# The first batch's mixing side by side, and the first block's second layer by halves of its weights

## The chip, the cores and the metric

The kernel runs on one core of one Trainium2 chip. The metric is device time of one launch, in microseconds (us). A core has TensorE (PE, matmuls; PEld are its weight loads), VectorE (DVE), ScalarE (ACT), GpSimd (POOL) and SyncE (SP, here only an issuer of transfers). Transfers between device memory and the on-chip buffer run on 16 DMA engines; in this kernel GpSimd issues the loads of inputs, SyncE the small ones and the outputs. TensorE writes its results to PSUM, eight banks of 128 partitions by 2 KB; VectorE and ScalarE copy them out.

## The reference

Attention with a few extra "beacon" keys per head, and on its output a mixing over the sequence of low rank (rank 32) followed by a two-layer network over the channels. Eight batches, eight heads of 64, 576 tokens, 16 beacons, 512 channels, 2048 in the hidden layer:

```python
k_all = np.concatenate([beacon_k, k], axis=2)
v_all = np.concatenate([beacon_v, v], axis=2)
scores = scale * np.matmul(q, k_all.transpose(0, 1, 3, 2))
causal[:, Nb:] = np.triu(np.ones((S, S), dtype=bool), k=1)
scores = np.where(causal, -1000000000.0, scores)
...
a /= a.sum(-1, keepdims=True) + 1e-09
x = np.matmul(a, v_all)            # heads side by side: (B, S, 512)
xt = x.transpose(0, 2, 1)
h = xt @ U @ V                     # U: 576 x 32, V: 32 x 576
u = x + h.transpose(0, 2, 1)
out = u + np.maximum(u @ w_ch1, 0.0) @ w_ch2
```

## The kernel before

*Tiling.* The 576 tokens of a batch are cut into five tiles (112, 128, 128, 128, 80 tokens), the 512 channels into four blocks of 128, the heads into four pairs per batch. Pairs are numbered through all batches: 0 to 3 are the first batch's, 4 to 7 the second's, 8 to 11 the third's. The network runs over blocks of 512 rows of the (8 x 576) rows; the first block therefore lies wholly in the first batch.

*Attention.* For a pair, q and k are regrouped on VectorE into a tile `pr` (`regroup`, copies at L268, the beacons at L270), turned by TensorE (`tps`, L275 or L281), copied out of PSUM into `qT` and `kT` (L308, L313), multiplied into scores (`sps`, L348 or L382), exponentiated by ScalarE (`expt`), masked by VectorE and multiplied with V of the attention (`po`, L397). VectorE then writes the normalised result into `xb` (L405, L406).

*Mixing.* The head of the mixing multiplies U with `xb` into `qtp` (32 rows of rank by channels), VectorE copies that to an f16 tile, and the correction multiplies it with V. The results accumulate in PSUM upon the turned x (`ups` for tokens 0 to 495, `uend` for the last 80) and are copied into `uT`, channels by tokens. For batches from the second on (`mix_units`) all four channel blocks stand side by side: the head writes them into four column groups of 32 (L434), and the correction reads them in four row groups of 32 (L459). For that `Vsb` holds V four times, in rows 0, 32, 64 and 96 on, and `Vend` the last 80 columns of V in one row group per block, with zeros elsewhere. The first batch has its own `first_mix` (L481), which does the blocks in two sets, 0 and 1, then 2 and 3: `head(c0, n)` takes both blocks of a set as one matmul of 256 columns per token tile (L489); `begin` brings the turned x into PSUM; `rest` multiplies each block with V (L506) and copies out.

*Small inputs.* `small_loads` (L162) lets SyncE read U and V as f32 into one tile. `cast`, called later, lets GpSimd write them as f16 (`Usb`, L176; `Vsb`, L177); SyncE then copies V to the other row groups (L181) and its end into `Vend` (L182). GpSimd issues the loads of the second batch, of w1 (four quarters) and of w2 (two halves, L195) around that call, in the order of the code, and then the third batch's loads (`load_batch(2)`).

*Network.* `mlp_units` makes a list of steps for a block of 512 rows: 16 g-steps (first layer, `gps`, L534, one PSUM bank each, relu out to `gT`) and then 16 c-steps (second layer, `cps`, L560): step (i, part) multiplies rows i x 128 on with four of the sixteen hidden slices; four parts fill a bank, the fourth is followed by the copy `ob` (VectorE for even i in the first block, L577, ScalarE for odd i, L575) and the transfer out. Hidden slices 0 to 7 read the first half of w2, 8 to 15 the second.

*Order.* The order of the work on each engine is that of the code (`manual_schedule`, L808), written out by hand. The steps of the network stand in a list, `queue`, and `fill(n)` takes n off it between pieces of attention ("f" in the lines of `play` takes one). After the second batch's attention, `mix(1)` puts the second batch's mixing among the 16 c-steps of the first block: head, c-step, corrections (`most`), three c-steps, end part, and from then on a c-step and an empty place by turns for four c-steps. Then come, at L905 to L909: eight steps of the queue, the regrouping of pairs 8 and 9 (six copies on VectorE, which need the third batch's k and q), eight more steps, and a line that begins with the turning of pair 8's q, a step, the turning of its k, a step, and pair 8's scores.

Of the kernel before, what the change touches and what calls it, by code (L numbers as in the profile page):

```python
# [11 lines left out]
F32 = mybir.dt.float32  # L12
# [6 lines left out]
P = 128  # L19
# [11 lines left out]
def kernel(  # L31
# [13 lines left out]
    nc = tc.nc  # L45
    B, H, S, D = q.shape
    Nb = beacon_k.shape[2]
    DM = H * D
    R = moe_U.shape[1]
# [12 lines left out]
    nq = [min(S, P * (j + 1) - Nb) - q0[j] for j in range(NC)]  # L62
    NT = NC
    QM, NL = q0[NT - 1], nq[NT - 1]
# [97 lines left out]
    def small_loads():  # L162

        f = utp.tile([P, NT * R + S], F32, name="small", tag="ut")
        nc.vector.memset(f[0:1, 0:1], 0.0)
        uf, vf = f[:, 0 : NT * R].rearrange("p (j r) -> p j r", r=R), f[0:R, NT * R :]
        nc.sync.dma_start(out=uf[: nq[0], 0, :], in_=moe_U[0 : nq[0], :])
        nc.sync.dma_start(
            out=uf[:, 1 : NT - 1, :], in_=moe_U[q0[1] : QM, :].rearrange("(j p) r -> p j r", p=P)
        )  # L170
        nc.sync.dma_start(out=uf[:NL, NT - 1, :], in_=moe_U[QM:S, :])
        nc.sync.dma_start(out=vf, in_=moe_V)

        def cast():
            for rr, jj in ((nq[0], slice(0, 1)), (P, slice(1, NT - 1)), (NL, slice(NT - 1, NT))):
                nc.gpsimd.tensor_copy(out=Usb[:rr, jj, :], in_=uf[:rr, jj, :])  # L176
            nc.gpsimd.tensor_copy(out=Vsb[0:R, :], in_=vf)  # L177
            for cc in range(NCC):
                rs = ds(R * cc, R)
                if cc:  # L180
                    nc.sync.dma_start(out=Vsb[rs, :], in_=Vsb[0:R, :])  # L181
                nc.sync.dma_start(out=Vend[rs, cc, :], in_=Vsb[0:R, QM:S])  # L182

        return cast

# [295 lines left out]
    def first_mix(xb):  # L481

        qts = outp.tile([P, DM], F16, name="qfirst", tag="ob")
        cell = {}

        def head(c0, n):
            qtp = pst([R, P * n], F32, name="qtp")
            for j in range(NT):
                nc.tensor.matmul(  # L489
                    qtp, Usb[: nq[j], j, :], xb[: nq[j], j, ds(P * c0, P * n)], start=(j == 0), stop=(j == NT - 1)  # L490
                )
            nc.vector.tensor_copy(out=qts[0:R, ds(P * c0, P * n)], in_=qtp)
            emptying(qtp)

        def begin(c0, cs, n=2):
            for cc in cs:
                cell[cc] = pst([P, QM], F32, name="ups")
                x_into(xb, cell[cc], cc, list(range(NT - 1)), 0, True)
                if cc == c0:
                    cell["end"] = pst([P, n, NL], F32, name="uend")  # L500
                x_into(xb, cell["end"][:, cc - c0, :], cc, [NT - 1], QM, cc == c0)

        def rest(c0, n, copies, end):
            for at in (0, QM):
                for i in range(n):
                    nc.tensor.matmul(  # L506
                        cell["end"][:, i, :] if at else cell[c0 + i], qts[0:R, ts(c0 + i, P)],
                        Vsb[0:R, at : S if at else QM], start=False, stop=True, skip_group_check=True,
                    )
            for cc, copy in zip(range(c0, c0 + n), copies):  # L510
                copy(out=uT[:, cc, 0:QM], in_=cell[cc])
                emptying(cell[cc])
            end(out=uT[:, ds(c0, n), QM:S], in_=cell["end"])
            emptying(cell["end"])

        return head, begin, rest

    def mlp_units(t0, n, dst, flip, turned=True, last=False):


        units = []
        gT = {}
        held = {}

        def turn():
            ut = utp.tile([P, 4, DM], F16, name="ut", tag="ut")
            for cc in range(NCC):
                nc.sync.dma_start_transpose(out=ut[:, :, ts(cc, P)], in_=uT[:, cc, ds(t0, 4 * P)])
            gT["u"] = ut

        def g_part(dc, upto):
            g, done = held.get(dc) or (pst([P, 512], F32, name="gps"), 0)
            for cc in range(done, upto):
                nc.tensor.matmul(  # L534
                    g[:, 0:n], w1[:, cc, ts(dc, P)], uT[:, cc, ds(t0, n)], start=(cc == 0), stop=(cc == NCC - 1)
                )
            held[dc] = g, upto

        def g_unit(dc):
            if dc == 0:  # L540
                gT["t"] = gtp.tile([P, NDC, 512], F16, name="gT", tag="gT")
                if turned:
                    turn()
            g_part(dc, NCC)
            g, _ = held.pop(dc)
            if (dc % 3 if not turned else (dc + flip) % 2 or dc in (5, 6, 7)):
                nc.scalar.activation(out=gT["t"][:, dc, 0:n], in_=g[:, 0:n], func=AF.Relu)  # L547
            else:
                nc.vector.tensor_scalar_max(out=gT["t"][:, dc, 0:n], in0=g[:, 0:n], scalar1=0.0)  # L549
            emptying(g)  # L550

        cps = {}

        def c_unit(i, part):
            m = min(P, n - P * i)
            if part == 0:
                cps["t"] = pst([P, DM], F32, name="cps")
            ps = cps["t"]
            for dc in range(4 * part, 4 * part + 4):
                nc.tensor.matmul(  # L560
                    ps[:m, :], gT["t"][:, dc, ds(P * i, m)], w2[:, dc, :], start=(dc == 0),
                    stop=turned and dc == NDC - 1, skip_group_check=True,
                )
            if part == 3:
                ob = outp.tile([P, DM], F32, name="ob", tag="ob")
                if not turned:
                    for cc in range(NCC):
                        nc.tensor.matmul(
                            ps[:m, ts(cc, P)], uT[:, cc, ds(t0 + P * i, m)], ident, start=False, stop=True,
                            skip_group_check=True,  # L570
                        )
                if turned:
                    nc.vector.tensor_tensor(out=ob[:m, :], in0=ps[:m, :], in1=gT["u"][:m, i, :], op=ALU.add)  # L573
                elif i % 2:
                    nc.scalar.activation(out=ob[:m, :], in_=ps[:m, :], func=AF.Copy)  # L575
                else:
                    nc.vector.tensor_copy(out=ob[:m, :], in_=ps[:m, :])  # L577
                emptying(ps)
                nc.sync.dma_start(out=dst(i, m), in_=ob[:m, :])

        def c_half(i, part):
            hs = ds(DM // 2 * (part // 2), DM // 2)
            if part % 2 == 0:
                cps["t"] = pst([P, DM // 2], F32, name="cph")
            for dc in range(NDC // 2 * (part % 2), NDC // 2 * (part % 2 + 1)):
                nc.tensor.matmul(  # L586
                    cps["t"], gT["t"][:, dc, ts(i, P)], w2[:, dc, hs], start=(dc == 0), stop=(dc == NDC - 1)
                )
            if part % 2:
                ob = outp.tile([P, DM // 2], F32, name="oh", tag="ob")  # L590
                nc.vector.tensor_tensor(out=ob, in0=cps["t"], in1=gT["u"][:, i, hs], op=ALU.add)
                emptying(cps["t"])
                nc.sync.dma_start(out=dst(i, P)[:, hs], in_=ob)

        units += [lambda dc=dc: g_unit(dc) for dc in range(NDC)]
        for i in range((n + P - 1) // P):
            c = c_half if last and i == n // P - 1 else c_unit
            units += [lambda i=i, part=part, c=c: c(i, part) for part in range(4)]
        return units, g_part


# [206 lines left out]
    with tc.manual_schedule(engines={ENG.PE, ENG.Activation, ENG.DVE, ENG.SP, ENG.Pool}):  # L808
# [60 lines left out]
        head, begin, rest = first_mix(xbs[0])  # L869
        feed(0)  # L870
        part = state["part"]
# [7 lines left out]
        rest(0, 2, (act_copy, act_copy), act_copy)  # L879
        av = av_of(3)  # L880
        av[0]()
        av[1]()
        begin(2, (2,))
        part(D0, 2)
        part(D1, 2)
        head(2, 2)
# [100 lines left out]
        for p in range(NP1, NP):  # L987
            b, c = divmod(p, NH2)
# [78 lines left out]
    with tc.If(n_bad != 0, label="general"):  # L1067
        with tc.For_i(0, B, 1) as bi:
            L = qk_tiles()
            qT = qkt.tile([P, NH2, S], F16, name="qT", tag="qT")  # L1070
            xb = xbp.tile([P, NT, DM], F16, name="xb", tag="xb")
# [11 lines left out]
            for t0 in range(0, S, 512):  # L1083
                n = min(512, S - t0)
# [32 lines left out]
```

## Time and profile before

| | |
|---|---|
| median of 3 runs | 350.42 us (349.91 to 350.76) |
| the profiled execution's own time | 350.22 us |
| its span, first to last instruction | 348.6 us |
| TensorE busy | 341.6 us, 98% |
| VectorE, ScalarE, GpSimd busy | 190.5, 163.5, 98.0 us |
| moved by the DMA engines | 41.88 MB |

A profile is of one execution. Rows of the chain give start, length and what; rows of a timeline give start, length, engine, line, operation, output and inputs, shape and count, and in brackets how long the engine had been idle and what ended that. Lines (L...) are those of the kernel's file. Ends of matmuls are modelled, so a row's length reaches a little beyond the next start; differences of starts are safer.

### The profile page before, as it was taken

The page shows a single profiled execution, that of the slowest core. Times are in us where ns is not written, and L with a number is a line of the kernel's source. Part 1 is how long each engine was busy: PE and PEld are TensorE (multiplying, and loading weights), DVE is VectorE, ACT ScalarE, POOL GpSimd, SP SyncE. Part 2 cuts the span into 40 slices and gives each one's busy share as a digit, 9 for nine tenths or more (in the row PEclk, how much of TensorE's full clock was granted, in tenths as well). Part 3 has the DMA queues.
Part 4 walks back from the last instruction along what each step waited for, and adds up shares of the span by engine and source line. Part 5 has one row for each costly group of instructions (what it writes and reads, how often), then busy time and mean ns, then how long its engine had stood idle before and what let it go on. Part 6 is the DMA issues. An engine that isn't in the chain of part 4 may idle for free.

```text
span 348.6 us, 7792 instructions
## 1 busy us (share of the span) xinstructions
PE 341.6 (98%) x3084; PEld 173.0 (50%) x3084; DVE 190.5 (55%) x492; ACT 163.5 (47%) x358; POOL 98.0 (28%) x137
## 2 busy tenths in 40 slices
PE   8999999999999999999999999999999999999995
PEld 3565564555554455444554545445445444444443
DVE  5776964789875653654565456535655542323311
ACT  5957851578823665167614753494434203302300
POOL 8885713653505547303830140000000000000000
PEclk9999999999999999999999999999999999999999
DMA  9999999999999999991999799613123314013011
GB/s 168 128 181 182 157 196 181 222 145 144 131 147 144 159 152 127 172 190 8 141 134 192 124 107 132 179 44 68 63 75 47 68 63 120 2 60 105 17 65 65
DMA packets 146635, 41.88 MB, mean 120 GB/s; under 512 B 131488, under 2 KB 142080, under 8 KB 146592
## 3 DMA queue, kind: packets, MB, share of 16 engines
q0 software_dynamic: 87440, 18.18, 71.6%
q1 hardware_dynamic: 58928, 22.84, 36.3%
q8 instruction: 26, 0.43, 0.6%
q10 hardware_dynamic: 224, 0.30, 0.3%
q14 instruction: 17, 0.14, 0.2%
HBM read 37.37 MB, written 9.44 MB: 134 GB/s over the span
## 4 chain that ended last, share of the span: by engine, by line
PE 88%; DMA 7%; DVE 2%; ACT 1%; issue 0%; POOL 0%
PE gps L534 35%; PE cps L560 33%; PE po L397 8%; PE sps L382 6%; DMA st<-in_q_dram 6%; ACT expt L354 1%; PE tps L275 1%; PE sps L348 1%; PE cph L586 1%; DMA stq<-in_q_dram 1%; PE qtp L434 1%; PE tps L281 1%; DVE qT L308 1%; DVE pr L268 1%; PE ups L459 1%; DVE kT L308 0%
## 5 line engine op out<-in xcount | busy, mean ns | idle before, releaser
L534 PE MATMUL gps<-uT,w 128*128 128x512 f16 x576 | 136.0, 379 | 0.1
L560 PE MATMUL cps<-w,gT 128*128 128x512 f16 x560 | 130.9, 379 | 0.1
L388 ACT ACTIVATE expt<-sps 128x496 f16<-128x496 f32 x192 | 82.5, 534 | 71.6 <-PE sps L382 71.6
L547 ACT ACTIVATE gT<-gps 128x512 f16<-128x512 f32 x86 | 50.9, 622 | 78.8 <-PE gps L534 78.7
L534 PEld LDWEIGHTS <-w 128*128 128x128 f16 x576 | 51.8, 98 | 58.0 <-issue 2.4
L560 PEld LDWEIGHTS <-gT 128*128 128x128 f16 x560 | 50.9, 98 | 59.4 <-issue 6.5
L549 DVE TENSOR_SCALAR gT<-gps 128x512 f16<-128x512 f32 x58 | 39.9, 690 | 41.6 <-PE gps L534 39.9
L573 DVE TENSOR_TENSOR ob<-cps,ut 128x512 f32<-128x512 f32 x31 | 21.4, 691 | 48.3 <-PE cps L560 47.5
L218 POOL DMA_DIRECT2D vs<-in_v_dram x50 | 39.6, 807 | 17.0 <-PE po L397 4.8
L397 PEld LDWEIGHTS <-expt 128*128 128x128 f16 (+1 forms) x960 | 36.2, 98 | 12.8 <-issue 1.0
L397 PE MATMUL po<-vs,expt 128*128 128x65 f16 (+1 forms) x960 | 38.9, 194 | 0.1
L406 DVE TENSOR_TENSOR xb<-po,rec 128x320 f16<-128x320 f32 x64 | 31.5, 491 | 2.2
L324 DVE TENSOR_TENSOR expt<-expt,bigmask 128x512 f16<-128x512 f16 x58 | 24.3, 418 | 6.7 <-ACT expt L388 6.7
L354 ACT ACTIVATE expt<-sps 128x496 f16<-128x496 f32 (+1 forms) x64 | 27.0, 606 | 0.7 <-PE sps L348 0.6
L405 DVE RECIPROCAL rec<-po 128x5 f32<-128x5 f32 x64 | 12.1, 188 | 26.9 <-PE po L397 26.6
L382 PE MATMUL sps<-qT,kT 64*128 64x80 f16 (+4 forms) x288 | 23.3, 281 | 0.1
L200 POOL DMA_DIRECT2D vs<-in_beacon_v_dram x8 | 4.3, 536 | 57.2 <-PE po L397 57.2
L646 POOL DMA_DIRECT2D st<-in_q_dram x20 | 16.9, 863 | 7.2 <-DMA vs<-in_v_dram 4.3
L382 PEld LDWEIGHTS <-kT 64*128 64x128 f16 x288 | 9.8, 94 | 18.3 <-issue 14.4
L646 POOL DMA_DIRECT2D st<-in_k_dram x20 | 16.9, 868 | 3.3 <-DMA st<-in_q_dram 2.9
L446 DVE TENSOR_TENSOR uT<-ups,uT 128x496 f16<-128x496 f32 x24 | 14.5, 667 | 5.0 <-PE ups L459 5.0
L308 DVE COPY qT<-tps 128x576 f16<-128x576 f16 (+1 forms) x16 | 11.8, 735 | 3.5 <-PE tps L281 2.3
(97 smaller groups left out, 162.4 us busy)
## 6 DMA issues: line engine op xcount, KB each, us to landing
out_dram<-ob SPq DMA_DIRECT2D x35, 256.0 KB, 2.3
vs<-in_v_dram POOLq DMA_DIRECT2D x18, 128.0 KB, 7.3
w<-in_moe_w_ch_dram POOLq DMA_DIRECT2D x4, 512.0 KB, 6.9
w<-in_moe_w_ch_dram POOLq DMA_DIRECT2D x2, 1024.0 KB, 14.3
st<-in_k_dram POOLq DMA_DIRECT2D x12, 128.0 KB, 8.9
st<-in_q_dram POOLq DMA_DIRECT2D x12, 128.0 KB, 9.4
st<-in_k_dram POOLq DMA_DIRECT2D x2, 576.0 KB, 13.1
st<-in_q_dram POOLq DMA_DIRECT2D x2, 576.0 KB, 15.9
```

The source lines that it names most:

```text
L218: nc.gpsimd.dma_start(out=dst[a : a + nq[j], j, :, :], in_=src[hs, ds(q0[j], nq[j]), :].rearrange("h p d -> p h d"))
L324: nc.vector.tensor_tensor(out=e4, in0=e4, in1=bigmask, op=ALU.min)
L354: nc.scalar.activation(out=ex[i][:, ds(SLOT * g, gw[g])], in_=ps[g, i][:, 0 : gw[g]], func=AF.Exp, scale=scale)
L382: nc.tensor.matmul(ps[p, g, i][:, ds(o, w)], kT[hp, c, ds(P * ch, P)], qT[hp, c, ds(qa, w)], start=True, stop=True,)
L388: nc.scalar.activation(out=at[p][3][i][:, ds(SLOT * g, gw[g])], in_=ps[p, g, i][:, 0 : gw[g]], func=AF.Exp, scale=scale)
L397: nc.tensor.matmul(po[:, j, :], ex[0 : nk[c], ds(blk[(c, j)], P)], vs[0 : nk[c], ds(c * H * E + h * E, E)], start=(c == 0), stop=(c == j),)
L406: nc.vector.tensor_tensor(out=xb[:, :, ds(h * D, D)], in0=po[:, :, 0:D], in1=r.broadcast_to([P, NT, D]), op=ALU.mult)
L534: nc.tensor.matmul(g[:, 0:n], w1[:, cc, ts(dc, P)], uT[:, cc, ds(t0, n)], start=(cc == 0), stop=(cc == NCC - 1))
L547: nc.scalar.activation(out=gT["t"][:, dc, 0:n], in_=g[:, 0:n], func=AF.Relu)
L549: nc.vector.tensor_scalar_max(out=gT["t"][:, dc, 0:n], in0=g[:, 0:n], scalar1=0.0)
L560: nc.tensor.matmul(ps[:m, :], gT["t"][:, dc, ds(P * i, m)], w2[:, dc, :], start=(dc == 0), stop=turned and dc == NDC - 1, skip_group_check ...
L646: nc.gpsimd.dma_start(out=dst[a : m[j], j, :, :], in_=src[:, ds(q0[j], nq[j]), :].rearrange("h p d -> p h d"))
```

## The change

Four edits.

- *V in 64 rows.* V is read twice from device memory, into rows 0 to 31 and 32 to 63 of the f32 tile; GpSimd casts 64 rows at once, and writes `Vend` for blocks 0 and 1 with two casts of its own. SyncE's copies remain for blocks 2 and 3 only.
- *The first batch's mixing.* In a set, the two blocks' heads go into two column groups of 32 (ten matmuls of 128 columns in the place of five of 256), the copy out is 64 by 128, the corrections read row group i for block i, and the end part takes all 64 rows against `Vend`.
- *An order.* The turned x of block 2 is begun between the two attention products of pair 3 and not behind them.
- *The first block's second layer.* Of the 16 c-steps the first eight come in another order: parts 0 and 1 of rows 0, parts 0 and 1 of rows 1, parts 2 and 3 of rows 0, parts 2 and 3 of rows 1. Two PSUM banks are then open at a time.

```diff
-        uf, vf = f[:, 0 : NT * R].rearrange("p (j r) -> p j r", r=R), f[0:R, NT * R :]
+        uf, vf = f[:, 0 : NT * R].rearrange("p (j r) -> p j r", r=R), f[0 : 2 * R, NT * R :]
...
-        nc.sync.dma_start(out=vf, in_=moe_V)
+        for i in range(2):
+            nc.sync.dma_start(out=vf[ds(R * i, R), :], in_=moe_V)
...
-            nc.gpsimd.tensor_copy(out=Vsb[0:R, :], in_=vf)
+            nc.gpsimd.tensor_copy(out=Vsb[0 : 2 * R, :], in_=vf)
             for cc in range(NCC):
                 rs = ds(R * cc, R)
-                if cc:
+                if cc > 1:
                     nc.sync.dma_start(out=Vsb[rs, :], in_=Vsb[0:R, :])
-                nc.sync.dma_start(out=Vend[rs, cc, :], in_=Vsb[0:R, QM:S])
+                    nc.sync.dma_start(out=Vend[rs, cc, :], in_=Vsb[0:R, QM:S])
+                else:
+                    nc.gpsimd.tensor_copy(out=Vend[rs, cc, :], in_=vf[rs, QM:S])
...
         def head(c0, n):
-            qtp = pst([R, P * n], F32, name="qtp")
+            qtp = pst([R * n, P], F32, name="qtp")
             for j in range(NT):
-                nc.tensor.matmul(
-                    qtp, Usb[: nq[j], j, :], xb[: nq[j], j, ds(P * c0, P * n)], start=(j == 0), stop=(j == NT - 1)
-                )
-            nc.vector.tensor_copy(out=qts[0:R, ds(P * c0, P * n)], in_=qtp)
+                for i in range(n):
+                    nc.tensor.matmul(
+                        qtp[ds(R * i, R), :], Usb[: nq[j], j, :], xb[: nq[j], j, ts(c0 + i, P)],
+                        start=(j == 0), stop=(j == NT - 1), skip_group_check=True, tile_position=(0, R * i),
+                    )
+            nc.vector.tensor_copy(out=qts[0 : R * n, ts(c0, P)], in_=qtp)
...
         def rest(c0, n, copies, end):
-            for at in (0, QM):
-                for i in range(n):
-                    nc.tensor.matmul(
-                        cell["end"][:, i, :] if at else cell[c0 + i], qts[0:R, ts(c0 + i, P)],
-                        Vsb[0:R, at : S if at else QM], start=False, stop=True, skip_group_check=True,
-                    )
+            for i in range(n):
+                nc.tensor.matmul(
+                    cell[c0 + i], qts[ds(R * i, R), ts(c0, P)], Vsb[ds(R * i, R), 0:QM],
+                    start=False, stop=True, skip_group_check=True,
+                )
+            for i in range(n):
+                nc.tensor.matmul(
+                    cell["end"][:, i, :], qts[0 : R * n, ts(c0, P)], Vend[0 : R * n, i, :],
+                    start=False, stop=True, skip_group_check=True,
+                )
...
-        for i in range((n + P - 1) // P):
+        turns = [(i, part) for i in range((n + P - 1) // P) for part in range(4)]
+        if not turned and n == 512:
+            turns[0:8] = [(i, part) for h in (0, 2) for i in (0, 1) for part in (h, h + 1)]
+        for i, part in turns:
...
         av[0]()
+        begin(2, (2,))
         av[1]()
-        begin(2, (2,))
         part(D0, 2)
```

The bank of a c-step (`c_unit`, L554) is kept per i (`cps[i]`) and no longer under one name.

More of the change, by code (lines that the diff above doesn't have):

```diff
@@ L556, in c_unit @@
             if part == 0:
-                cps["t"] = pst([P, DM], F32, name="cps")
-            ps = cps["t"]
+                cps[i] = pst([P, DM], F32, name="cps")
+            ps = cps[i]
             for dc in range(4 * part, 4 * part + 4):
@@ L595, in mlp_units @@
         units += [lambda dc=dc: g_unit(dc) for dc in range(NDC)]
-        for i in range((n + P - 1) // P):
+        turns = [(i, part) for i in range((n + P - 1) // P) for part in range(4)]
+        if not turned and n == 512:
+            turns[0:8] = [(i, part) for h in (0, 2) for i in (0, 1) for part in (h, h + 1)]
+        for i, part in turns:
             c = c_half if last and i == n // P - 1 else c_unit
-            units += [lambda i=i, part=part, c=c: c(i, part) for part in range(4)]
+            units.append(lambda i=i, part=part, c=c: c(i, part))
         return units, g_part
```

## The prediction

> **What bounds the kernel now.** I read the page first, then the chain of work that ended last between 11 and 66 us, then the timelines of TensorE, VectorE and GpSimd and the DMA view around its pieces. The page (engine: busy us, share of the span, instructions):
>
> ```profile
> span 348.6 us, 7792 instructions
> PE 341.6 (98%) x3084; PEld 173.0 (50%) x3084; DVE 190.5 (55%) x492; ACT 163.5 (47%) x358; POOL 98.0 (28%) x137
> ```
>
> TensorE is the bound over the whole, so TensorE work that is saved should come off the end, unless a wait stands between. The chain (start us, length us, what) shows one:
>
> ```profile
> 18.88 0.65 PE qtp L489 x5
> ...
> 20.62 0.52 PE ups L506 x2
> 21.14 0.07 PE uend L506 x2
> ...
> 23.36 0.65 PE qtp L489 x5
> ...
> 24.81 0.52 PE ups L506 x2
> ...
> 38.90 20.70 DMA st<-in_q_dram
> ...
> 61.05 0.67 DVE qT L308
> ...
> 62.53 0.58 PE sps L382 x4
> ```
>
> The pieces of the first batch's mixing stand at 18.9 to 25.3. Then comes the load of the third batch's q: issued at 38.90, landed 20.70 later, at 59.6. From there VectorE works without a pause (the regrouping of pairs 8 and 9, the copies of qT and kT out of PSUM) until the scores of pair 8 start at 62.53. So what is saved before 59.6 has to get past that landing. How tight it is, from the timelines of TensorE and VectorE (start, length, engine, line; a length holds the modelled end of the last matmul, so I use differences of starts):
>
> ```profile
> 49.29 0.61 PE L434 MATMUL qtp<-xb,Usb 112*32 112x128 f16 x20
> 49.84 1.04 PE L560 MATMUL cps<-w,gT 128*128 128x512 f16 x4
> ...
> 51.69 0.39 PE L459 MATMUL ups<-Vsb,qts 32*128 32x496 f16 x4
> 52.01 2.98 PE L560 MATMUL cps<-w,gT 128*128 128x512 f16 x12
> ...
> 59.02 1.03 PE L560 MATMUL cps<-w,gT 128*128 128x512 f16 x4
> 60.04 0.43 PE L275 MATMUL tps<-ident,pr 96*128 96x96 f16 x6
> ...
> 61.44 1.03 PE L560 MATMUL cps<-w,gT 128*128 128x512 f16 x4
> ```
>
> ```profile
> 55.26 0.69 DVE L577 COPY ob<-cps 128x512 f32<-128x512 f32 x1 [1.86 <-PE cps L568]
> 55.86 0.48 DVE L448 CAST uT<-uend 128x320 f16<-128x320 f32 x1
> 56.26 0.35 DVE L268 COPY pr<-st 96x768 f16<-96x768 f16 x1
> ...
> 59.63 0.62 DVE L268 COPY pr<-st 96x768 f16<-96x768 f16 x2 [2.80 <-DMA st<-in_q_dram]
> ```
>
> The four matmuls from 59.02 are streamed by about 59.9 (four of the 12 from 52.01 take about 0.9); the transposes of pair 8's q start at 60.04, once the copy behind the landing is done. TensorE thus arrives only some 0.15 us ahead of the load: two paths in balance. VectorE sat 2.80 us idle before that copy, and the row "x2" at 59.63 holds, behind the q copy, the k copy of pair 9, whose data came with pair 8's k (copied at 56.26): VectorE takes nothing out of the order of the code.
>
> **The change, part by part.** *Heads* (two sets of two blocks). Before: five matmuls of 256 columns, 0.65 each set. After: ten of 128 columns in two column groups. Nearest row: 20 in four groups go from 49.29 to the next start at 49.84, 0.55, so ten take about 0.3. Saved 0.35 a set, 0.7 in all; between 0, if the groups do not run side by side, and 0.75.
>
> *Corrections* by V. Before 0.52 + 0.07 a set, two 496-column matmuls one after the other. After, in two row groups: the four of L459 take 51.69 to 52.01, 0.32, so 0.3 plus two short end matmuls over 64 rows, about 0.4. Saved 0.15 a set, 0.3 in all; between 0 and 0.5. The Trainium skill ("TensorEngine Tiling (Array Packing)", Key Properties) has a rule against this: a change of tiling mode drains the array, and the end part now goes from 32-row to 64-row tiles before the 128-row work. No row here parts that drain from the rest; by the rule the saving shrinks, and the sum below stays as it is, since this lies ahead of the landing.
>
> *Narrower copy of q (64x128) and the block of channels 256 to 383 begun one step earlier.* Five matmuls change place with 15, so TensorE's total is the same; a wait on the mask or the q copy may go. I count 0 to 0.1.
>
> *Second layer by halves of w2.* The issue of w2's halves and the landing of the second:
>
> ```profile
> 35.80 1.81 POOL L195 DMA_DIRECT2D w<-in_moe_w_ch_dram  x2
> ```
>
> ```profile
> w<-in_moe_w_ch_dram POOLq DMA_DIRECT2D x1, 1024.0 KB, 16.4
> ```
>
> The second issue starts about 0.9 into the first row, so its 16.4 end near 53.1. Before, the third unit of the first block, which reads that half, comes second in the 12 matmuls from 52.01, whose 2.98 is some 0.2 more than three times four. After, it comes two units (1.7 us) later: 0.2 saved, and room for an earlier arrival.
>
> Together TensorE is ready for pair 8's q about 1.2 us earlier (0.3 to 1.6). Its cover is the q load: TensorE stands idle from about 58.8 until the copy at 59.63 is through, and the gain at the end is **0**. If the load landed earlier by x, up to 1.2 of it would count.
>
> *The price of the halves.* The first block's output copy (L577, VectorE) needs its fourth unit. That unit moves from fourth to sixth place, and so out of the first eight steps of the queue into the second eight. Between the two stand the six regrouping copies of pairs 8 and 9. VectorE's order becomes: regroup 8, its q copy waiting for the load, regroup 9, then the output copy, then qT. What was done at 55.26 in idle time now lies in the unbroken stretch from 59.63 to 62.53, and qT, kT and the scores at 62.53 wait for it. Its worth is the step from 55.26 to the next start at 55.86, **+0.60** (0 if the load is early enough for VectorE to reach it in time, 0.69 at most). TensorE loses the same: its unit from 61.44 is streamed by 62.3, and the scores are next in order. Behind them the chain is TensorE's to the end, so nothing gives it back. SyncE's output transfer of that block, and of the second block queued behind it, go with the copy; four output buffers stand behind them, so I count 0.
>
> *V in 64 rows.* GpSimd's rows, the rates of the queues over 12.5 to 14.5 us (packets, MB, share of 16 engines; q0 holds GpSimd's loads, q1 SyncE's), and SyncE's transfers (KB, us to landing):
>
> ```profile
> 16.11 0.53 POOL L176 CAST Usb<-small 128x96 f16<-128x96 f32 x2 [1.07 <-DMA small<-in_moe_U_dram]
> 16.68 0.66 POOL L177 CAST Vsb<-small 32x576 f16<-32x576 f32 x1
> 17.30 0.69 POOL L203 DMA_DIRECT2D st<-in_k_dram  x1
> ```
>
> ```profile
> q0 software_dynamic: 1250, 0.21, 136.4%
> q1 hardware_dynamic: 515, 0.13, 33.1%
> ```
>
> ```profile
> Vsb<-Vsb SPq DMA_DIRECT2D x3, 36.0 KB, 6.2
> small<-in_moe_V_dram SPq DMA_DIRECT2D x1, 72.0 KB, 5.2
> ```
>
> Added: a second V read, 72 KB; GpSimd's V cast waits for it (0 to 0.5) and two small casts follow (0.53 for two such), so its next load leaves 0.5 to 1.0 later than 17.30, and every load behind it in that queue too. Removed: one 36 KB copy and two of 5 KB, 46 KB. At 0.34 MB in 2 us the 26 KB more are 0.15 us; that later landing I add, **+0.15**. Bounds: -0.3 (only the removed 46 KB count) and +0.9 (the queue runs dry for GpSimd's whole delay). I stay near the low end, as q0 holds more than a full share (136.4%) and so has work in stock. The Trainium skill ("DMA: Bandwidth & Descriptors", Issuing engines are not separate DMA queues) says that transfers started by different engines interleave on the same 16 DMA engines; the two shares above, in one stretch, agree. By that rule the whole second read, 72 KB or 0.42, would lie ahead of GpSimd's loads, and the sum would be 0.27 higher.
>
> **Sum.** The profiled execution took 350.22 (span 348.6 and 1.6 around it). 350.22 + 0 + 0.60 + 0.15 = 350.97. It lay 0.20 under the median of the runs, 350.42 (349.91 to 350.76), so for a median I say **351.2**, 0.2% slower.
>
> **Rivals.** *The saving arrives (the other side).* Should the q load usually land 1.3 us or more before 59.6, VectorE is past the regrouping before TensorE needs it, the output copy falls into idle time again, and 1.2 comes off: 349.2. It turns at a landing 0.75 earlier (no change) and is clear at about 1.4. For it: TensorE is 98% busy, and 46 KB leave the queues. Against it: 46 KB are only 0.27 us at that rate, the load is queued behind all others since 38.90, and the fastest run, 349.91, is only 0.31 under the profiled one, about what TensorE lost to the two late spots at 60.04 and 62.53.
>
> *It does little.* The load lands some 0.3 to 0.6 earlier, or VectorE slips the output copy in: 350.4 to 350.9. For it: both paths are in balance, so 0.60 is the most that order can cost. Against it: the copy's place in the code, between regroup 9 and qT.
>
> *The loads run dry.* GpSimd's delay of up to 1.0 passes whole to the queue and to the q load: 350.22 + 0.60 + 0.9 + 0.20 = 351.9, with a further stall perhaps 352.3. For it: GpSimd waited for the U loads at 16.11 already, so the load at 17.30 is issued with little lead. Against it: the share of 136.4%.
>
> **How the numbers follow.** 0.2% (0.70 us) is about what a measurement of this kernel tells from no change: 349.7 and 351.1 are the bounds. Forecast 0.50, with its own range 350.8 to 351.6, of which two thirds lie beyond 351.1; saving arrives 0.14; does little 0.20; runs dry 0.16. Slower 0.33 + 0.16 = 0.49, same 0.17 + 0.20 = 0.37, faster 0.14. The range 350.0 to 352.3 leaves out most of the second case and the tail of the last.
>
> **What would show it.** Right: the two heads take about 0.3 and the corrections start side by side; the TensorE row at 52.01 has no stall in it; TensorE idles about 1 us ahead of pair 8's q transposes with VectorE's regrouping as releaser, that copy still starting at 59.4 to 60.2; the output copy L577 right behind the last regrouping copy, and the scores of pair 8 at 63.0 to 63.5 after an idle stretch of 0.6 or more. Wrong: the q load landing before 58.9, or a q transpose without wait (the saving arrives); the issue at 17.30 moved by over 1 us with the landing moved as far (runs dry); a stretch behind 63 us that is shorter or longer than before.

## The result, and the profile after

The changed kernel took **352.12 us** (median of 11 runs, 351.02 to 354.44) beside 350.48 (11 runs, 349.91 to 350.88): ratio 1.0048, 95% interval 1.0034 to 1.0062, so 1.64 us **slower**. Timed again in a later comparison it took 351.66 beside 350.38, ratio 1.0041 (1.0025 to 1.0057). Its profiled execution took 352.71, 2.49 more than that of before (350.22). That execution lies on the long side of its runs, which matters below. The page:

```profile
span 351.1 us, 7814 instructions
...
PE 341.8 (97%) x3094; PEld 173.0 (49%) x3094; DVE 190.3 (54%) x492; ACT 163.8 (47%) x358; POOL 98.4 (28%) x139
```

TensorE is busy for 341.8 us, 0.2 more than before: the time came as waiting, and the chain that ended last shows where (start us, length us, what):

```profile
11.90 5.35 DMA small<-in_moe_V_dram
...
17.37 0.66 POOL Vsb L178
18.03 0.40 POOL Vend L185
...
18.48 0.24 POOL Vend L185
18.73 1.30 POOL st L206 x2
...
21.96 10.47 DMA st<-in_q_dram
...
32.71 3.68 POOL vs L221 x5
...
40.17 20.56 DMA st<-in_q_dram
...
61.82 0.36 DVE pr L271
62.18 0.60 DVE ob L586
62.77 0.67 DVE qT L311
...
64.23 0.58 PE sps L385 x4
```

Two things are new in it. It now begins with the second read of V, on which GpSimd waits, then casts three times, and only then issues the loads of the second batch; GpSimd's later issues, that of the third batch's q among them, hang on the landing of one of these. And the output copy of the first block (L586) stands between the regrouping and the copies of qT and kT. The load of the third batch's q lands at 60.73 (59.61 before), and the scores of pair 8 start at 64.23 (62.53 before): +1.70, of which 1.12 is the load and 0.58 the copy. TensorE's timeline (start, length, line; in brackets the idle time before and what ended it):

```profile
15.61 0.45 PE L284 MATMUL tps<-ident,st 96*64 96x96 f16 x12 [0.18 <-DMA st<-in_q_dram]
...
19.25 0.46 PE L493 MATMUL qtp<-xb,Usb 112*32 112x128 f16 x10 [0.23 <-DVE xb L409]
19.64 0.63 PE L400 MATMUL po<-vs,expt 128*128 128x65 f16 x15
...
20.72 0.38 PE L510 MATMUL ups<-Vsb,qfirst 32*128 32x496 f16 x2
21.04 0.24 PE L515 MATMUL uend<-Vend,qfirst 64*128 64x80 f16 x2
21.21 0.63 PE L400 MATMUL po<-vs,expt 128*128 128x65 f16 x15
...
25.07 0.40 PE L284 MATMUL tps<-ident,st 96*64 96x96 f16 x10
25.86 0.50 PE L284 MATMUL tps<-ident,st 112*64 112x112 f16 x14 [0.39 <-DMA st<-in_beacon_k_dram]
26.29 3.19 PE L543 MATMUL gps<-uT,w 128*128 128x512 f16 x14
```

The kernel before, at the last of these:

```profile
25.33 0.71 PE L281 MATMUL tps<-ident,st 96*64 96x96 f16 x24
25.98 3.19 PE L534 MATMUL gps<-uT,w 128*128 128x512 f16 x14
```

The changed kernel further on:

```profile
52.35 2.76 PE L569 MATMUL cps<-w,gT 128*128 128x512 f16 x12
...
59.15 1.03 PE L569 MATMUL cps<-w,gT 128*128 128x512 f16 x4
61.17 0.43 PE L278 MATMUL tps<-ident,pr 96*128 96x96 f16 x6 [1.00 <-DVE pr L271]
...
64.23 0.58 PE L385 MATMUL sps<-qT,kT 64*128 64x496 f16 x4 [0.64 <-DVE kT L316]
...
78.88 0.42 PE L278 MATMUL tps<-ident,pr 96*128 96x96 f16 x6 [0.38 <-DVE gT L558]
```

The mixing is shorter: a head is 0.39 (19.25 to 19.64) for 0.66 (18.81 to 19.47 before), a set's corrections 0.49 (20.72 to 21.21) for 0.59 (20.55 to 21.14 before). Two sets save 2 x 0.26 + 2 x 0.10 = 0.73 (from unrounded starts). The wait on w2's second half is gone as well (2.76 for 2.98 at 52.35). But TensorE was already 0.32 later at 15.61, most of it by waiting for the first batch's last q; it waited for xb at 19.25; and at 25.86 it waits for the second batch's key beacons. At 25.07 it stood 0.26 ahead of the kernel before all the same; behind the beacons, at 26.29, it is 0.31 late. Its last group ahead of pair 8's q starts at 59.15, against 59.02 before.

GpSimd's timeline shows why the beacons are late:

```profile
15.94 0.44 POOL L177 CAST Usb<-small 128x96 f16<-128x96 f32 x2 [0.92 <-DMA small<-in_moe_U_dram]
17.37 0.66 POOL L178 CAST Vsb<-small 64x576 f16<-64x576 f32 x1 [1.00 <-DMA small<-in_moe_V_dram]
17.98 0.74 POOL L185 CAST Vend<-small 32x80 f16<-32x80 f32 x2
18.68 0.68 POOL L206 DMA_DIRECT2D st<-in_k_dram  x1
```

The V cast waits 1.00 for the second read of V, the two casts for Vend take 0.74 more, and the k load goes out at 18.68 (17.30 before), 1.38 later. Did GpSimd's queue have enough work in stock to bridge that? Its packets, MB and share of the 16 engines from 19 to 21 us, first before, then after:

```profile
q0 software_dynamic: 430, 0.33, 114.8%
```

```profile
q0 software_dynamic: 88, 0.07, 38.3%
```

It had not: the queue moved a fifth of what it had moved before. And the delay is handed on. In both traces GpSimd's loads take eight semaphores by turns, and each waits for the landing of the load eight places ahead of it. So the second batch's last q lands at 32.43 (31.23 before), GpSimd's next issue comes at 32.71, and the third batch's q goes out at 40.17 (38.90 before), 1.27 later. The kernel before at the same place:

```profile
31.51 3.58 POOL L218 DMA_DIRECT2D vs<-in_v_dram  x5 [1.37 <-DMA st<-in_q_dram]
```

The rest of the 2.49 lies behind 64 us: 0.53 at the transposes at 78.88, where TensorE waits for VectorE, and 0.26 behind the last matmul. VectorE's rows, first of the changed kernel, then of the kernel before:

```profile
76.46 0.66 DVE L271 COPY pr<-st 96x768 f16<-96x768 f16 x1
77.16 0.68 DVE L273 COPY pr<-st 16x128 f16<-16x128 f16 x1
```

```profile
74.76 0.35 DVE L268 COPY pr<-st 96x768 f16<-96x768 f16 x1
75.13 0.47 DVE L270 COPY pr<-st 16x128 f16<-16x128 f16 x1
```

The same two copies took 0.52 longer in this execution. In the profile of e12, the same kernel run again, they took 0.34 and 0.44 and TensorE did not wait there. So this part doesn't come with every execution of the changed kernel (more on it at e3).

### The profile page after: what moved, and what is told of

It is laid out like the page before. It is cut to its first block, busy times and chain, and to the rows that moved or that the text cites. A ratio compares the mean times of both kernels' runs of the same rounds, so it can differ in the third digit from the quotient of the medians.

```text
span 351.1 us, 7814 instructions
## 1 busy us (share of the span) xinstructions
PE 341.8 (97%) x3094; PEld 173.0 (49%) x3094; DVE 190.3 (54%) x492; ACT 163.8 (47%) x358; POOL 98.4 (28%) x139
## 4 chain that ended last, share of the span: by engine, by line
PE 81%; DMA 10%; POOL 3%; DVE 3%; SPq 0%; issue 0%; POOLq 0%
PE cps L569 32%; PE gps L543 31%; DMA st<-in_q_dram 9%; PE po L400 6%; PE sps L385 6%; DMA small<-in_moe_V_dram 2%; PE tps L278 1%; PE idle L253 1%; POOL vs L221 1%; PE cph L595 1%; POOL st L206 1%; PE qtp L437 1%; DVE qT L311 1%; PE ups L462 1%; DVE pr L271 1%; POOL w L198 1%
## 5 line engine op out<-in xcount | busy, mean ns | idle before, releaser
L658 POOL DMA_DIRECT2D st<-in_q_dram x20 | 16.8, 861 | 7.6 <-DMA vs<-in_v_dram 2.6
L658 POOL DMA_DIRECT2D st<-in_k_dram x20 | 16.9, 875 | 5.1 <-DMA st<-in_q_dram 3.6
L449 DVE TENSOR_TENSOR uT<-ups,uT 128x496 f16<-128x496 f32 x24 | 14.5, 668 | 5.0 <-PE ups L462 4.4
```

The source lines that it names most:

```text
L658: nc.gpsimd.dma_start(out=dst[a : m[j], j, :, :], in_=src[:, ds(q0[j], nq[j]), :].rearrange("h p d -> p h d"))
```

## The experiments

Three causes were to be told apart: the **late issue** of GpSimd's loads (by the wait for V and the two casts), the **copy** of the first block behind the regrouping, and the **second read** of V by itself; and beside them, whether the mixing's saving counts at all. The runs were made in three comparisons (e1 to e4, e5 to e8, e9 to e12). "k issued" is GpSimd's first load of the second batch, "q landed" that of the third batch, "scores" those of pair 8, all in us in the one profiled execution.

| run | median | before | ratio (95%) | k issued | q landed | scores |
|---|---|---|---|---|---|---|
| before | | | | 17.30 | 59.61 | 62.53 |
| after | 352.12 | 350.48 | 1.0048 (1.0034 to 1.0062) | 18.68 | 60.73 | 64.23 |
| e1 | 351.25 | 350.66 | 1.0020 (1.0010 to 1.0031) | 18.65 | 61.95 | 64.87 |
| e2 | 351.17 | 350.66 | 1.0017 (0.9997 to 1.0038) | 17.05 | 60.36 | 63.86 |
| e3 | 351.07 | 350.66 | 1.0020 (1.0004 to 1.0035) | 16.76 | 58.33 | 62.26 |
| e4 | 351.38 | 350.66 | 1.0010 (0.9981 to 1.0039) | 17.22 | 57.80 | 62.03 |
| e5 | 351.49 | 350.50 | 1.0020 (1.0001 to 1.0038) | 18.84 | 60.88 | 63.81 |
| e6 | 352.03 | 350.50 | 1.0026 (1.0008 to 1.0044) | 19.01 | 61.84 | 64.77 |
| e7 | 350.42 | 350.50 | 0.9996 (0.9983 to 1.0008) | 14.70 | 57.83 | 62.37 |
| e8 | 349.75 | 350.50 | 0.9975 (0.9963 to 0.9987) | 14.71 | 57.08 | 61.74 |
| e9 | 350.17 | 350.38 | 0.9997 (0.9983 to 1.0010) | 14.92 | 56.73 | 62.16 |
| e10 | 349.87 | 350.38 | 0.9983 (0.9972 to 0.9995) | 14.76 | 57.29 | 62.94 |
| e11 | 349.91 | 350.38 | 0.9990 (0.9972 to 1.0007) | 14.93 | 57.76 | 61.74 |
| e12 | 351.66 | 350.38 | 1.0041 (1.0025 to 1.0057) | 18.41 | 60.78 | 64.29 |

The ratios, with their intervals, carry the argument; they aren't the quotients of the two medians beside them (e6's medians alone would give 1.0044, e4's 1.0021). Each interval is 0.10% to 0.29% to either side, so a difference of two ratios is known to about 0.2%. The landing of one profiled execution carries less: it scatters by more than 1 us (e1 and e5 issue the third batch's q at 40.09 and 40.08 and it lands 1.07 apart). As a group the profiles do part: the five with k out at 18.41 or later (after, e1, e5, e6, e12) issue that q at 40.08 to 41.05, and it lands at 60.73 to 61.95; the four with k out at 16.76 to 17.30 (before, e2, e3, e4) issue it at 38.07 to 39.70, and it lands at 57.80 to 60.36.

**e1: the change without its new order of the second layer.**

```
         turns = [(i, part) for i in range((n + P - 1) // P) for part in range(4)]
-        if not turned and n == 512:
-            turns[0:8] = [(i, part) for h in (0, 2) for i in (0, 1) for part in (h, h + 1)]
```

> The changed kernel with the c-steps of the first block in the old order. Theory: the changed kernel pays twice, 1.1 us for the later landing of the third batch's q (60.73 against 59.61) and 0.60 for the output copy behind the regrouping. Then the copy is back at about 55, the landing stays at 60.4 to 60.9, pair 8's scores start near 63.6, and the time is 0.8 to 1.2 us above the kernel before. Rival: the late landing is only one profile's draw and the copy's place is the whole cause; then the landing is near 59.7 and the time within 0.3 us of the kernel before. Second rival: the saved 1.2 us of TensorE come through once the copy is gone: 0.5 us or more faster.

Measured: +0.20%, against +0.41% and +0.48% for the whole change. The output copy is back in VectorE's idle time (it starts at 56.03), and the scores follow the q landing by 2.92, as before (62.53 - 59.61), instead of 3.50. So the order costs 0.2 to 0.3% (give or take 0.2%), and the rest of the change is slower without it too.

**e2: the new order alone, in the kernel before.**

```
-                cps["t"] = pst([P, DM], F32, name="cps")
+                cps[i] = pst([P, DM], F32, name="cps")
...
+            turns[0:8] = [(i, part) for h in (0, 2) for i in (0, 1) for part in (h, h + 1)]
```

> The kernel before with only the new order of the first block's c-steps. Theory: the loads stay as they were (q lands at 59.4 to 59.8), the output copy stands behind the last regrouping copy, pair 8's scores start near 63.1 and the time is 0.5 to 0.7 us above the kernel before. Rival: VectorE's copy is covered, and the wait for w2's second half (0.2 us) goes: 0 to 0.2 us faster.

Measured: +0.17%, with an interval that just reaches no change. VectorE's timeline shows the mechanism without the rest of the change:

```profile
60.38 0.62 DVE L268 COPY pr<-st 96x768 f16<-96x768 f16 x2 [2.67 <-DMA st<-in_q_dram]
...
61.72 0.68 DVE L577 COPY ob<-cps 128x512 f32<-128x512 f32 x1
62.32 0.74 DVE L308 COPY qT<-tps 128x576 f16<-128x576 f16 x1
```

The copy stands behind the last regrouping copy and holds qT back by 0.60. The wait on w2 is gone here too (0.22 less), and it brings nothing: TensorE waits 0.96 for pair 8's q all the same.

**e3: the change, with the casts of V behind the two loads.**

```
         token_load(nc.gpsimd, q[1], qt, HALVES[0])
+        cast_v()
         key_beacons(nc.gpsimd, beacon_k[1], kt, ALLH)
```

> The changed kernel with GpSimd's V casts (and their wait for the second V read) behind the two loads of the second batch's k and q, and no longer ahead of them. The second read and the order of steps stay. Theory 'late issue' (the load queue runs dry while GpSimd waits and casts): k's load is issued near 17.0, the third batch's q lands at 59.4 to 59.9, and 0.5 to 0.8 us over the kernel before are left, for the output copy. Rival 'bytes' (the 72 KB of the second read delay everything behind): the landing stays at 60.4 or later and the time 1.4 to 1.8 us above the kernel before.

Measured: +0.20%, half of what the change cost. The loads go out at 16.76, and the q load lands early enough (58.33) that the copy is done by 60.3 and the scores start at 62.26. So the late issue is the other half. It isn't all: with the loads at least as early as before, the kernel is still no faster than before. In its profile the copy costs nothing, and the 0.79 that this execution took longer than the one before lies behind 64 us: pair 8's scores come 0.27 earlier, then TensorE loses 0.64 at 77.02, where it waits for VectorE as in the changed kernel at 78.88, and 0.32 are behind the last matmul. The profiles of e4 and e11 lose 0.46 and 0.41 at that place, e6 0.16, all others at most 0.1. All four with a large loss read V twice, but three versions that read it twice (e1, e5, e12) don't have it; whether the read has to do with it isn't shown.

**e4: the kernel before, with a second read of V that nobody uses.**

```
         nc.sync.dma_start(out=vf, in_=moe_V)
+        nc.sync.dma_start(out=f[R : 2 * R, NT * R :], in_=moe_V)
```

> The kernel before with a second read of V into rows that nobody reads, so without a wait and without casts. Theory 'late issue': GpSimd's k load leaves at 17.2 to 17.5 as before, the third batch's q lands within 0.2 of 59.6, the time within 0.3 us of the kernel before. Rival 'bytes': 72 KB at 170 GB/s, 0.4 us, on the landing and on the time.

Measured: 1.0010, interval 0.9981 to 1.0039: inconclusive. The first batch's last q landed at 15.10 (14.23 before). Over all profiles it landed at 14.05 to 15.71 in the seven with a second read, in the middle 15.52, and at 13.30 to 15.43 in the seven without, in the middle 14.23; so the read seems to delay the transfers beside it, though not in each execution, and its worth at the end isn't told apart from nothing.

**e5: the change, with the first block's output copy on ScalarE.**

```
-                elif i % 2:
+                elif i < 2 or i % 2:
                     nc.scalar.activation(out=ob[:m, :], in_=ps[:m, :], func=AF.Copy)
```

> The changed kernel with the first block's first output copy on ScalarE, so that VectorE has nothing between the last regrouping copy and the copy of qT. Theory (the copy costs 0.60): pair 8's scores start 2.9 us after the q landing or behind TensorE's own work, as in the kernel before, and the time is 0.5 to 0.7 us less than the changed kernel's, 0.8 to 1.1 us above the kernel before. Rival (the copy is covered in most executions): no change from the changed kernel, 1.5 us above the kernel before.

Measured: +0.20%, so taking the copy off VectorE recovers 0.2 to 0.3% (give or take 0.2%), the same as undoing the order (e1). VectorE goes from the last regrouping copy at 61.98 straight to qT at 62.25, and the scores follow the landing by 2.93. The order is dear only by where that copy falls.

**e6: the kernel before, with the V cast done three times.**

```
-            nc.gpsimd.tensor_copy(out=Vsb[0:R, :], in_=vf)
+            for _ in range(3):
+                nc.gpsimd.tensor_copy(out=Vsb[0:R, :], in_=vf)
```

> The kernel before with GpSimd's V cast done three times over, 1.3 us more ahead of the load of the second batch's k; nothing else. Theory 'late issue': k's load leaves near 18.6 and lands 1 to 1.8 later than 22.1, the beacons near 25.8, the third batch's q on average 1 us later, and the time is 0.5 to 1.0 us above the kernel before. Rival: the load queue has enough in stock; no difference.

Measured: +0.26%. Nothing but GpSimd's time ahead of the loads is changed here (its three casts take 2.39, and k goes out at 19.01, 1.71 later), so the late issue by itself costs 0.26% (0.08 to 0.44%), or 0.9 us. No byte was added, and the queue runs as empty from 19 to 21 us as in the changed kernel:

```profile
q0 software_dynamic: 85, 0.06, 39.0%
```

TensorE's timeline names where the delay arrives in this profile:

```profile
28.84 1.04 PE L535 MATMUL gps<-uT,w 128*128 128x512 f16 x4 [0.19 <-DMA w<-in_moe_w_ch_dram]
...
45.12 1.04 PE L535 MATMUL gps<-uT,w 128*128 128x512 f16 x4 [0.91 <-DMA w<-in_moe_w_ch_dram]
```

The load of q isn't the only one with little to spare: two quarters of w1 come too late as well, and w2's second half (a wait of 0.58 at 55.38).

**e7: the kernel before, with all casts behind the two loads.**

```
         emit_w1(0)
-        cast()
         Ls[1] = qk_tiles()
...
         token_load(nc.gpsimd, q[1], qt, HALVES[0])
+        cast()
         key_beacons(nc.gpsimd, beacon_k[1], kt, ALLH)
```

> The kernel before with all of GpSimd's casts of U and V behind the loads of the second batch's first k and q halves, so these leave at about 14.8 and not at 17.3. Theory 'late issue': even the kernel before loses a little there; the landings come 0.3 to 0.8 earlier and the time falls by 0 to 0.3 us, no more, since TensorE's own work ends at 59.9. Rival: the loads collide with the last V loads of the first batch, TensorE waits for these, and the time rises by 0.3 us or more.

Measured: 0.9996, no difference. The loads go out 2.6 earlier and the q of the third batch lands at 57.83, but pair 8's transposes start at 59.89 (60.04 before): TensorE gets there no earlier by itself. The two paths are in balance, as the prediction had them: loads that are later cost, loads that are earlier alone bring nothing.

**e8: the change with its costs taken out.** The copy goes to ScalarE as in e5, the second read is dropped (GpSimd casts the same 32 rows twice), all casts stand behind the two loads, and w1's last quarter is loaded ahead of the second batch's last V.

```
-        for i in range(2):
-            nc.sync.dma_start(out=vf[ds(R * i, R), :], in_=moe_V)
+        nc.sync.dma_start(out=vf, in_=moe_V)
...
+            for i in range(2):
+                nc.gpsimd.tensor_copy(out=Vsb[ds(R * i, R), :], in_=vf)
...
-        v_tokens(v[1], vss[1], HALVES[1])
         emit_w1(3)
+        v_tokens(v[1], vss[1], HALVES[1])
```

> The changed kernel with the costs taken out: the first block's first output copy on ScalarE, no second V read (GpSimd casts the same 32 rows twice), all casts behind the two loads, and w1's last quarter issued ahead of the second batch's last V loads. Theory: TensorE keeps about 0.7 of mixing and 0.2 of w2's wait, the loads land no later than before, and the time is 0.3 to 0.9 us under the kernel before. Rival: the third batch's q, whose landing is set by the bytes ahead of it, holds the end at the time of the kernel before, within 0.3 us.

Measured: **349.75 beside 350.50, ratio 0.9975 (0.9963 to 0.9987)**: faster than both kernels. Its GpSimd and TensorE timelines:

```profile
14.71 0.75 POOL L206 DMA_DIRECT2D st<-in_k_dram  x1
15.38 0.75 POOL L206 DMA_DIRECT2D st<-in_q_dram  x1
16.05 0.82 POOL L176 CAST Usb<-small 112x32 f16<-112x32 f32 x3
16.82 1.46 POOL L178 CAST Vsb<-small 32x576 f16<-32x576 f32 x2
```

```profile
58.40 1.03 PE L569 MATMUL cps<-w,gT 128*128 128x512 f16 x4
59.26 0.42 PE L278 MATMUL tps<-ident,pr 96*128 96x96 f16 x6
...
61.74 0.58 PE L385 MATMUL sps<-qT,kT 64*128 64x496 f16 x4
```

GpSimd no longer waits for anything between 13 and 19 us, and TensorE takes up pair 8's q without a wait, 0.78 earlier than in the kernel before. There the saving reaches the end.

**e9: e8 with the mixing and the small inputs of the kernel before.**

```
-            qtp = pst([R * n, P], F32, name="qtp")
+            qtp = pst([R, P * n], F32, name="qtp")
...
-                    cell[c0 + i], qts[ds(R * i, R), ts(c0, P)], Vsb[ds(R * i, R), 0:QM],
+                        cell["end"][:, i, :] if at else cell[c0 + i], qts[0:R, ts(c0 + i, P)],
```

> The combined version with the first batch's mixing and small inputs as in the kernel before (loads first, w1's last quarter early, new step order, output copy on ScalarE stay). Theory: with the loads early, what TensorE saves in the mixing counts: this one is 0.4 to 0.8 us slower than the combined version, which is 0.0 to 0.4 us under the kernel before. Rival: the earlier loads gave it all; same time as the combined version.

Measured: 0.9997 beside e8's 0.9975, a difference of 0.22% (give or take 0.18%), or 0.8 us, where the 0.73 counted above is 0.21%. (The two ran in different comparisons, each beside the kernel before.) So with the waits out of the way the mixing is worth about what TensorE saves by it, and without it the other edits of e8 aren't told from nothing, as in e7.

**e10: e8 with the first block's copy on VectorE again.**

```
-                elif i < 2 or i % 2:
+                elif i % 2:
```

> The combined version with the first output copy back on VectorE, behind the six regrouping copies. Theory: it costs only because the q load is late; with the landing near 57 VectorE is done with the regrouping before TensorE gets there, and the time is that of the combined version, 0.5 to 0.9 us under the kernel before, at most 0.2 more. Rival: the copy's place costs 0.6 whatever the loads do: near the kernel before.

Measured: 0.9983, still faster than before. VectorE's timeline:

```profile
58.38 0.35 DVE L271 COPY pr<-st 96x768 f16<-96x768 f16 x1
58.66 0.68 DVE L586 COPY ob<-cps 128x512 f32<-128x512 f32 x1
60.92 0.76 DVE L311 COPY qT<-tps 128x576 f16<-128x576 f16 x1 [1.59 <-PE tps L278]
```

The copy has the same place in the order as in the changed kernel, but the load landed at 57.29, so it is followed by 1.59 of idle time and delays nothing. The same order costs 0.2 to 0.3% where the load is late, and where it is early the medians differ by 0.08% (0.9983 beside 0.9975), which the intervals don't tell from nothing: the two costs are not independent. (Pair 8's scores are later in this profile, 62.94, because TensorE itself comes there later: its transposes start at 60.47, for 59.26 in e8. It lost that at the start, where the same matmuls took longer in this execution, so that it stood 1.36 later already at 14.64; why isn't shown. The execution, 350.85, was the longest of the eleven. With TensorE 1.21 earlier, 0.38 of the idle time would be left.)

**e11: e8 with the second read of V.**

```
-        nc.sync.dma_start(out=vf, in_=moe_V)
+        for i in range(2):
+            nc.sync.dma_start(out=vf[ds(R * i, R), :], in_=moe_V)
...
-            for i in range(2):
-                nc.gpsimd.tensor_copy(out=Vsb[ds(R * i, R), :], in_=vf)
+            nc.gpsimd.tensor_copy(out=Vsb[0 : 2 * R, :], in_=vf)
```

> The combined version with the second read of V back in the place of GpSimd's second cast. Theory: the read alone is worth little; the first batch's last q load lands up to 1 us later, near 15, for up to 0.3 us, so the time is 0 to 0.3 us above the combined version. Rival 'bytes': 0.4 us or more above it.

Measured: 0.9990 (0.9972 to 1.0007) beside e8's 0.9975 (0.9963 to 0.9987). The intervals overlap, so this too doesn't tell the read's own cost from nothing. The first batch's last q landed at 15.71 (14.22 in e8). With e4 (1.0010), both point to about 0.1% and neither shows it.

**e12: the changed kernel again.** No edit.

> The changed kernel itself, a second time and beside the others. Theory: k's load issued near 18.7, the third batch's q landing on a later side of 60, the copy behind the regrouping; 1.2 to 2.0 us above the kernel before. Rival: the first measurement was a bad draw of the loads; within 0.7 us of the kernel before.

Measured: +0.41% beside +0.48%: the result stands. In this profile the k load goes out at 18.41, the output copy stands at 62.15 and the scores at 64.29, as in the first one, and there is no wait at the transposes of about 78 us. From 19 to 21 us the queue's share is 51.5%, and TensorE waits 0.46 for the key beacons and 0.48 for a quarter of w1.

**Taken together.** Of the change's +0.41 to +0.48%, the place of the copy accounts for 0.2 to 0.3% (e1 and e5 recover it, e2 has it alone) and the late issue for as much (e3 recovers it, e6 has it alone); each share is known to about 0.2% only. The mixing saves 0.2% only where TensorE and not a load sets the start of pair 8 (e8 and e9). Left open are the second read's own share and, with it, the 0.2% that e3 keeps.

## Why the prediction was right and wrong

The direction was right and the mechanism of the copy too; the time lies inside the range, near its upper end, 0.9 us above the likeliest 351.2 and outside that case's own range (350.8 to 351.6). What came is the sum of the rival **the loads run dry** (351.9 to 352.3), to which I gave 0.16. That the measured time lies inside the range is owed to that rival; the sum itself missed 0.9.

- *Heads*: predicted 0.35 a set, measured 0.26. The row of L434 has 20 matmuls in four column groups; ten in two groups take 0.39, not half of 0.55: 0.039 for each matmul in place of 0.028. Width of the grouping, and not only the number of matmuls, sets the time.
- *Corrections*: predicted 0.15, measured 0.10. The two do start together (20.721 and 20.725 in the trace, one row "x2" in the timeline), but the end part over 64 rows starts 0.32 behind them (20.72 to 21.04). The Trainium skill ("TensorEngine Tiling (Array Packing)", Key Properties) says that a change of tiling mode drains the array. The gap of 0.32 is no longer than that of the four L459 before (51.69 to 52.01), but there too the mode changes behind it, to 128 rows. Before, two one after the other took 0.43 (20.55 to 20.98), so one alone is some 0.22 by my estimate, and two side by side cost 0.1 more than one. Whether that is a drain isn't shown, as no run takes the change of mode away.
- *w2 by halves*: predicted 0.2, measured 0.22. Right, and hidden as foreseen (e2).
- *TensorE about 1.2 us earlier at pair 8*: wrong, it was 0.13 later. The step counted only what was saved. Later landings delayed TensorE twice ahead of that point (the first batch's last q at 15.61, and the key beacons, which turned 0.26 ahead into 0.31 late), and it arrived with nothing in hand. The idle stretch of 1.00 ahead of the transposes, which I had named as a sign of the saving, came about by a later load: that sign did not tell the two apart.
- *The halves' price*: predicted +0.60, measured 0.58 in the profile; by the ratios 0.2 to 0.3%, 0.7 to 1.0 us (e1, e5). Right in place, in cause, and nearly in size. That an earlier load would make it free, the turning point of the first rival, is what e10 shows.
- *V in 64 rows*: **the step that failed.** I had GpSimd's delay (0.5 to 1.0; measured 1.38) and the bound of +0.9, and chose +0.15, because the queue "has work in stock". The share I read, 136.4%, was that of 12.5 to 14.5 us, ahead of the delay; where the delay bites, from 19 to 21 us, it falls from 114.8% to 38.3%, so the stock didn't reach. The delay was then handed on from landing to issue: 1.38 at the k load, 1.27 at the issue of the third batch's q, 1.12 at its landing. That is the sign I had named for "runs dry". e6 shows the price: delay alone, with no byte added, costs 0.26%, 0.9 us. On the way the beacons, w1's quarters and w2 have little to spare too (TensorE waited 0.39 for the beacons in the changed kernel, 0.19 and 0.91 for w1 in e6), so the delay reaches TensorE at whichever comes first. The delay was longer than foreseen as the V cast waited for the second read by 1.00, where I allowed 0 to 0.5. The 0.27 that came from the Trainium skill's rule on interleaving ("DMA: Bandwidth & Descriptors", Issuing engines are not separate DMA queues) rested on the bytes of the second read; one transfer beside it landed later in e4 (14.23 to 15.10), but the read's worth at the end isn't told apart from nothing in e4 and e11.
- *The saving arrives*: didn't come, and its condition, a load that usually lands earlier, was made by hand in e8, which is faster by 0.25%, 0.9 us where the rival had 1.2.

## What to carry to other kernels

Where a profile shows an engine and a load arriving together, count an edit on both sides: what is saved on the engine is worth nothing until the load is earlier, and what delays the load is paid for. A queue's share tells of its stock only for the stretch it was read in: look at the stretch behind the late issue. On an engine that both computes and issues transfers, ask of every small operation put ahead of an issue what it waits for; issuing first and computing second cost nothing here (e7), and the saving counted in a version that did so (e8). And an idle slot on a helper engine belongs to a place in its order: a copy moved behind a waiting copy loses it, unless what that copy waits for comes early (e10).

## What the runs showed of the hardware that was not expected

- VectorE's regrouping copies are slower while GpSimd issues transfers. Over the fourteen profiles all 103 copies of 96x768 that lay beside no such issue took 339 to 357 ns; of 149 beside one, 36 took more than 1.3 times the least, up to 791. The 16x128 copies took 190 to 193 ns without (58 of them), and 397 in the median and up to 693 with (68). The rows at 76.46 and 77.16 above are such a case, and TensorE paid 0.53 for it. The two go together; what they share isn't shown.
- 1.1 to 1.7 us of delay at GpSimd ahead of one load left its queue nearly without work for two microseconds: from 19 to 21 us its share was 38.3% to 51.5% in the five profiles with k out at 18.41 or later, and 100.9% to 122.4% in the four with k out at 16.76 to 17.30.
- The landing of a load doesn't follow from its own issue alone. In e7 the second batch's k went out 2.6 earlier, the third batch's q only 0.65 earlier, and that q landed 1.78 earlier. In e8, e9 and e10 that q went out 1.0 to 1.6 later than in the kernel before and landed 2.3 to 2.9 earlier: it took 16.8 to 16.9 in place of 20.7; w2's second half, issued ahead of it, had landed at 50.6 to 51.2 in place of 53.1.
